# A weight conversion's shift takes its count from a PSUM column

## The chip, the cores and the metric
The kernel runs on one core of a Trainium2 chip. The metric is the device time of one execution in microseconds (us), the median of three runs: 1470.43 (1469.66 to 1470.89).

## The reference
Attention over keys and values that are averaged over 8 positions, then two mixture-like feed-forward blocks without a router. Inputs: q, k, v of 8 x 8 heads x 576 x 64; the weights are 64-bit floats.

```python
k_p = k.reshape(B, H, Sp, 8, D).mean(axis=3)
v_p = v.reshape(B, H, Sp, 8, D).mean(axis=3)
scores = scale * q @ k_p.T ; scores -= max
attn = exp(scores); attn /= sum(attn) + 1e-9
x = attn @ v_p                       # 4608 tokens x 512
h = (x @ w1) * (x @ w2) @ w3         # 1024 wide
x = h @ w_out                        # 512 wide
h = x @ w_in                         # 2048 wide
out = (h / (1 + exp(-1.702 * h))) @ w_out2
```

## The kernel before
Products are made in three passes of a split number (a high and a low half; helpers `split`, lines 103 to 105, and `mm3`, lines 112 to 116). w3 and w_out are multiplied with each other first, so that the first block is (x w1)(x w2) times one matrix.

The weights come as 64-bit floats, read as pairs of 32-bit words, 128 x 512 of them in a tile of 512 KB. `Conv` (line 127) turns them into 32-bit floats: `load` issues the DMA of a tile on SP's queue; `step` (line 155) does one tile: ACT scales the high word (line 166) and the low word (line 168), DVE shifts the high word left by 3 (line 169), POOL adds the two as integers (line 172). Two steps later the tile's `done` runs (a `split`, for w3 behind four turns on TensorE, line 508). There are 72 steps. The first 40 (8 tiles of w_out, 16 of w3, 8 of w1, 8 of w2) write ACT's result into the tile `w` in SBUF (`cv`, four buffers). For the last 32 (w_in and w_out2, from the seventh block on) `self.ps` is set to two PSUM banks, and ACT's result lies there.

The attention runs in groups of two heads, 32 groups. For each: `g0` transposes k and q (lines 255, 256) and sums the keys, `g1` makes the scores (line 277) in two halves, each in a PSUM bank of its own, and subtracts the maximum (lines 282, 284), `g2` is the exponential, `g3` normalizes, `g4` turns the probabilities (for the first four groups on TensorE, lines 351 to 362) and splits them, `g6` makes the outputs (lines 380 to 391). Groups 1 and 3 use the banks acc[2] and acc[3], all others wk[2] and wk[3]: the second half of the scores fills columns 0 to 287 of wk[3], the turning columns 0 to 447, the outputs columns 0 to 287. The row factors of `g3` lie in the last columns of wk[2].

The program order: the loop at line 568 runs step i, then the w3 products of the tile of step i - 3, then from i = 4 on one `tick` of the attention. Counted from 0, with the parts that touch wk[3]: scores of group 0 behind step 5, turning of group 0 behind step 8, scores of group 2 behind step 9, outputs of group 0 behind step 10, turning of group 2 behind step 12, outputs of group 2 behind step 14, scores of group 4 behind step 18. Steps 28 to 39 follow two by two in the loop over f of the first block (line 618), with the scores of groups 5, 6, 7 behind steps 28, 32, 36 and the outputs of groups 4, 5, 6 behind steps 30, 34, 38. Tiles 1, 3, 7, 9 and 12 to 23 are those of w3; from tile 12 on each of them gives 12 products.

Tile order and waits between engines are set by a scheduler that orders each engine's queue by its own forecast, within the dependences that the program order gives. Shifts run on DVE in the order of the steps, so the k-th row of line 169 in time is step k.

Of the kernel before, what the change touches and what calls it, by code (L numbers as in the profile page):

```python
# [9 lines left out]
U32 = mybir.dt.uint32  # L10
I32 = mybir.dt.int32
AF = mybir.ActivationFunctionType
ALU = mybir.AluOpType
# [4 lines left out]
P = 128  # L18
T = 512
# [3 lines left out]
def pooled_attention_moe_moe2(  # L23
# [18 lines left out]
    nc = tc.nc  # L42
# [31 lines left out]
    held = {}  # L74
    acc = [ps_p.tile([P, T], F32, name=f"acc{i}", tag=f"bank{i}") for i in range(4)]
    wk = [ps_p.tile([P, T], F32, name=f"wk{i}", tag=f"bank{i + 4}") for i in range(4)]
    HU = 2 * P
    NP1 = NF2 // 2
    A11, A12, S1, S2, S3, S4, A21, A22 = range(8)
    win_d = [dr_p.tile([P, 8, 2, HU], F32, name=f"wind{f}", tag=f"wind{f}") for f in range(NP1)]  # L80
    wraw_d = [dr_p.tile([P, T], F32, name=f"wrawd{f}", tag=f"wrawd{f}") for f in range(NF2)]
    wu_d = [dr_p.tile([P, NP1, 2, HU], F32, name=f"wud{u}", tag=f"wud{u}") for u in range(8)]
    x2_d = [dr_p.tile([P, KM, T], F32, name=f"x2d{b}", tag=f"x2d{b}") for b in range(NB)]

    def take(shape=(P, 2, T), dtype=F32R):
        pool, i = free.pop(0)
        t = pool.tile(list(shape), dtype, name=f"s{i}", tag=f"s{i}")
        held[id(t)] = (t, pool, i)
        return t
# [5 lines left out]
    def give(*ts):  # L95
        for t in ts:
            if id(t) in held:
                free.append(held.pop(id(t))[1:])
# [28 lines left out]
    class Conv:  # L127
# [27 lines left out]
        def step(self):  # L155

            new = None
            if self.staged:
                t, turn, done = self.staged.pop(0)
                lo_w, hi_w = t[:, :, 0], t[:, :, 1]  # L160
                w = cv_p[0].tile([P, T], F32, name="cv", tag="cv", bufs=4)
                wu = w.bitcast(U32)

                e = self.ps[self.n % len(self.ps)] if self.ps else w
                self.n += 1
                nc.scalar.activation(
                    e, hi_w.bitcast(F32), AF.Prelu, scale=2.0 ** -112, alpha=-2.0 ** 32)
                nc.scalar.activation(lo_w.bitcast(I32), lo_w, AF.Copy, scale=2.0 ** -29)
                nc.vector.tensor_scalar(  # L169
                    out=wu, in0=e.bitcast(U32), scalar1=3, scalar2=None,  # L170
                    op0=ALU.logical_shift_left)
                nc.gpsimd.tensor_tensor(  # L172
                    out=w.bitcast(I32), in0=w.bitcast(I32), in1=lo_w.bitcast(I32), op=ALU.add)
                give(t)
                new = [w, turn, done]
            mid, old = self.line
            if mid and mid[1]:
                mid[0] = mid[1](mid[0])
            key = old[2](old[0]) if old else None
            self.line = [new, mid]  # L180
            self.load()
            return key
# [8 lines left out]
    with pa_ctx:  # L191
# [7 lines left out]
            out=mask[:, 0], in_=mask[:, 0], compare_op=ALU.is_gt, fill=0.0,  # L199
            base=SK, pattern=[[0, D]], channel_multiplier=-1)  # L200
        nc.gpsimd.affine_select(
            out=mask[:, 1], in_=mask[:, 1], compare_op=ALU.is_ge, fill=0.0,
# [8 lines left out]
        for t in s_ts:  # L211
# [6 lines left out]
            out=ident, in_=ident, compare_op=ALU.is_equal, fill=0.0,  # L218
# [244 lines left out]
        def units(f, u0, u1, w, eng):  # L463

            t = take((P, 2, 2, HU))
            v = w.rearrange("p (u m) -> p u m", u=2)
            nc.scalar.copy(t[:, :, 0], v)
            eng.tensor_tensor(out=t[:, :, 1], in0=v, in1=f32(t[:, :, 0]), op=ALU.subtract)
            nc.sync.dma_start(win_d[f][:, u0:u1 + 1], f32(t))
            give(t)  # L470
# [9 lines left out]
        def win_second(f):  # L480
            def done(w):
                h = hold[0]
                a11, a12 = h[:, :HU], h[:, HU:]
                a21, a22 = w[:, :HU], w[:, HU:]
                units(f, A21, A22, w, nc.gpsimd)
# [186 lines left out]
    with tc.tile_pool(name="pb", bufs=1, reuse_waits="tile") as pb, \  # L672
# [16 lines left out]
        def pull():  # L689
            if todo:  # L690
# [3 lines left out]
                if i:  # L694
                    t = pb.tile([P, 2, 2, HU], F32R, name="st", tag=f"st{i}")
                else:
# [219 lines left out]
        for pr in range(1, NPAIR + 1):  # L916
# [122 lines left out]
            for name, u in OUT:  # L1039
# [5 lines left out]
                if pr == NPAIR and name == "M3":  # L1045
# [8 lines left out]
                    for m, t0, n in ((1, 0, T // 2), (0, 0, T), (1, T // 2, T // 2)):  # L1054
                        c = slice(t0, t0 + n)
                        for fp, (g, w) in enumerate(gw):
# [4 lines left out]
                            out=U[m][:, c], in0=bs[m][1][:, c], in1=U[m][:, c], op=ALU.add)  # L1061
                        ts = slice(t0 // 32, (t0 + n) // 32)
                        nc.vector.transpose(
                            out=ot[:, ts, m],
# [74 lines left out]
```

## Time and profile before

| | |
|---|---|
| median of 3 runs | 1470.43 us |
| profiled execution, its own time | 1467.92 us |
| its span | 1466.0 us |
| TensorE (PE) busy | 1433.6 us (98%) |
| VectorE (DVE) busy | 986.1 us (67%) |
| ScalarE (ACT) busy | 694.5 us (47%) |
| GpSimd (POOL) busy | 488.2 us (33%) |
| granted TensorE clock, mean | 0.994 |
| chain that ended last | PE 91%, DVE 4%, POOL 2% |

Busy times are those of one profiled execution. A product's time in a row holds its pipeline, so that TensorE's rows overlap; the sum of an engine's busy time counts each moment once. In a row of the timeline the idle time before an instruction and who ended it stand in brackets.

### The profile page before, as it was taken

To read this page: it belongs to the slowest core of one execution; us is meant where nothing else is said; L and a number is where in the kernel's file an instruction comes from. 1 tells how busy PE (TensorE), PEld (TensorE's weight loads), DVE (VectorE), ACT (ScalarE), POOL (GpSimd) and SP (SyncE) were. 2 spreads that over 40 slices of the span, in tenths; PEclk is the share of its full clock that TensorE was granted. 3 is DMA by queue.
4 is the path that set the end of the run, shared out by engine and by line. 5 is a ranking of instruction groups with operands and counts; after the bars stand their busy time and mean duration, and the time that the engine had idled before them with its cause. 6 is when DMAs were issued, how large, how long until landed. Compare 5 with 4: busy or idle time off the path is not lost.

```text
span 1466.0 us, 19491 instructions
## 1 busy us (share of the span) xinstructions
PE 1433.6 (98%) x6560; PEld 1189.7 (81%) x6560; DVE 986.1 (67%) x1730; ACT 694.5 (47%) x1212; POOL 488.2 (33%) x589
## 2 busy tenths in 40 slices
PE   5979999999999999999999999999999999999998
PEld 4857888888888888888888888888888888888887
DVE  7778998878788887655646336783559354954554
ACT  7875344433333433366635335653455244534442
POOL 8789655554555555347643300000000000000000
PEclk9989999999999999999999999999999999999999
DMA  9992333323222221089869979877677766785665
GB/s 262 245 238 53 60 79 61 80 49 75 52 71 52 71 44 38 27 284 347 324 229 384 349 234 315 305 213 231 201 232 227 230 197 221 242 235 184 199 214 144
DMA packets 294499, 267.64 MB, mean 183 GB/s; under 512 B 201728, under 2 KB 226304, under 8 KB 294400
## 3 DMA queue, kind: packets, MB, share of 16 engines
q1 hardware_dynamic: 291680, 265.09, 60.4%
q10 hardware_dynamic: 2720, 1.31, 0.3%
q8 instruction: 52, 0.85, 0.2%
q14 instruction: 47, 0.39, 0.1%
HBM read 209.72 MB, written 56.62 MB: 182 GB/s over the span
## 4 chain that ended last, share of the span: by engine, by line
PE 91%; DVE 4%; POOL 2%; ACT 1%; DMA 1%; issue 1%; SPq 0%; DVEq 0%; POOLq 0%; ACTq 0%
PE bk L709 45%; PE wk L114 8%; PE wk L115 8%; PE wk L116 8%; PE acc L114 5%; PE acc L115 5%; PE acc L116 5%; PE wk L277 2%; DVE p L314 1%; PE bk L114 1%; PE bk L115 1%; PE bk L116 1%; POOL cv L172 1%; DVE s L105 1%; DVE cv L169 1%
## 5 line engine op out<-in xcount | busy, mean ns | idle before, releaser
L709 PE MATMUL bk<-mv,st 128*128 128x512 f32 (+1 forms) x1164 | 269.8, 385 | 0.0
L709 PE MATMUL bk<-xM,st 128*128 128x512 f32 x1104 | 261.8, 389 | 0.0
L709 PEld LDWEIGHTS bk<-mv,st 128*128 128x128 f32 x1164 | 215.4, 188 | 43.6
L709 PEld LDWEIGHTS bk<-xM,st 128*128 128x128 f32 x1104 | 207.3, 188 | 43.0
L114 PE MATMUL wk<-s,s 128*128 128x512 f32 x576 | 226.9, 396 | 3.4 <-DVE a L641 1.5
L116 PE MATMUL wk<-s,s 128*128 128x512 f32 x576 | 225.1, 392 | 2.1 <-DVE s L105 2.1
L115 PE MATMUL wk<-s,s 128*128 128x512 f32 x576 | 225.0, 391 | 0.0
L314 DVE STREAM_TRANSPOSE p<-s_t 32x160 f32<-32x160 f32 (+1 forms) x560 | 178.5, 319 | 10.3
L114 PE MATMUL acc<-s,s 128*128 128x512 f32 x352 | 134.2, 404 | 8.4 <-DVE s L105 5.4
L115 PE MATMUL acc<-s,s 128*128 128x512 f32 x352 | 140.7, 400 | 1.2 <-POOL s L105 1.1
L116 PE MATMUL acc<-s,s 128*128 128x512 f32 x352 | 140.1, 398 | 0.0
L114 PEld LDWEIGHTS wk<-s,s 128*128 128x128 f32 x576 | 108.4, 188 | 27.1 <-DVE a L641 2.4
L116 PEld LDWEIGHTS wk<-s,s 128*128 128x128 f32 x576 | 108.5, 188 | 24.8 <-DVE s L105 2.3
L115 PEld LDWEIGHTS wk<-s,s 128*128 128x128 f32 x576 | 108.5, 188 | 22.1 <-DVE s L391 0.4
L105 DVE TENSOR_TENSOR mv<-g,mv 128x1024 fp32r<-128x1024 f32 x80 | 97.8, 1222 | 31.0 <-ACT mv L104 29.0
L104 ACT CAST mv<-g 128x1024 fp32r<-128x1024 f32 x80 | 84.2, 1053 | 70.8 <-PE bk L709 70.4
L172 POOL TENSOR_TENSOR cv<-cv,s 128x512 int32<-128x512 int32 x72 | 97.7, 1365 | 28.0 <-DVE cv L169 18.7
L105 POOL TENSOR_TENSOR s<-a,s 128x512 fp32r<-128x512 f32 x56 | 72.3, 1291 | 82.7 <-ACT s L104 62.8
L638 ACT COPY a<-wk 128x512 f32<-128x512 f32 x72 | 42.1, 585 | 110.5 <-PE wk L116 89.9
L369 POOL TENSOR_TENSOR ph<-p,ph 128x576 fp32r<-128x576 f32 x32 | 45.7, 1428 | 128.9 <-ACT ph L368 126.3
L114 PEld LDWEIGHTS acc<-s,s 128*128 128x128 f32 x352 | 67.6, 193 | 23.6 <-ACT s L104 5.1
L115 PEld LDWEIGHTS acc<-s,s 128*128 128x128 f32 x352 | 67.7, 192 | 15.2 <-POOL s L105 2.3
(191 smaller groups left out, 2352.2 us busy)
## 6 DMA issues: line engine op xcount, KB each, us to landing
st<-wud SPq DMA_DIRECT2D x95, 512.0 KB, 4.1
st<-wind SPq DMA_DIRECT2D x70, 512.0 KB, 4.8
st<-wind SPq DMA_DIRECT2D x70, 256.0 KB, 3.9
s<-in_moe_w_dram SPq DMA_DIRECT2D x32, 512.0 KB, 6.4
wind<-s SPq DMA_DIRECT2D x32, 512.0 KB, 5.3
s<-in_moe_w_out_dram SPq DMA_DIRECT2D x24, 512.0 KB, 6.9
kr<-in_k_dram SPq DMA_DIRECT2D x128, 72.0 KB, 2.6
qr<-in_q_dram SPq DMA_DIRECT2D x128, 72.0 KB, 2.6
```

The source lines that it names most:

```text
L104: nc.scalar.copy(dst[:, 0], src)
L105: lo_eng.tensor_tensor(out=dst[:, 1], in0=src, in1=f32(dst[:, 0]), op=ALU.subtract)
L114: nc.tensor.matmul(o, a[:, 0, a_sl], b[:, 0, b_sl], start=first, stop=False)
L115: nc.tensor.matmul(o, a[:, 0, a_sl], b[:, 1, b_sl], start=False, stop=False)
L116: nc.tensor.matmul(o, a[:, 1, a_sl], b[:, 0, b_sl], start=False, stop=last)
L169: nc.vector.tensor_scalar(out=wu, in0=e.bitcast(U32), scalar1=3, scalar2=None, op0=ALU.logical_shift_left)
L172: nc.gpsimd.tensor_tensor(out=w.bitcast(I32), in0=w.bitcast(I32), in1=lo_w.bitcast(I32), op=ALU.add)
L277: nc.tensor.matmul(sc[half][:, i * KW:(i + 1) * KW], qT[:, sl(tt)], mov, start=True, stop=True)
L314: nc.vector.transpose(out=dst[:, :nt, 32 * c:32 * c + 32], in_=s_t[32 * c:32 * c + 32, :nt, 32 * r:32 * r + 32])
L369: nc.gpsimd.tensor_tensor(out=ph[:, 1], in0=s0, in1=f32(ph[:, 0]), op=ALU.subtract)
L638: nc.scalar.copy(a, pa_)
L709: nc.tensor.matmul(o, w[:, x, m], b[:, y], start=first and n == 0, stop=last and n == 2, skip_group_check=True)
```

## The change
Before the first step a column of the PSUM bank wk[3] (column 511) is filled with the integer 3. In the first 40 steps the shift of line 169 becomes an operation of two tensors: the tile in SBUF and this column, read again for all 512 elements. The last 32 steps keep the old form.

```diff
@@ -74,6 +74,8 @@
     held = {}
     acc = [ps_p.tile([P, T], F32, name=f"acc{i}", tag=f"bank{i}") for i in range(4)]
     wk = [ps_p.tile([P, T], F32, name=f"wk{i}", tag=f"bank{i + 4}") for i in range(4)]
+    three = wk[3][:, T - 1:].bitcast(U32)
+    nc.vector.memset(three, 3)
     HU = 2 * P
     NP1 = NF2 // 2
     A11, A12, S1, S2, S3, S4, A21, A22 = range(8)
@@ -166,9 +168,14 @@
                 nc.scalar.activation(
                     e, hi_w.bitcast(F32), AF.Prelu, scale=2.0 ** -112, alpha=-2.0 ** 32)
                 nc.scalar.activation(lo_w.bitcast(I32), lo_w, AF.Copy, scale=2.0 ** -29)
-                nc.vector.tensor_scalar(
-                    out=wu, in0=e.bitcast(U32), scalar1=3, scalar2=None,
-                    op0=ALU.logical_shift_left)
+                if self.ps:
+                    nc.vector.tensor_scalar(
+                        out=wu, in0=e.bitcast(U32), scalar1=3, scalar2=None,
+                        op0=ALU.logical_shift_left)
+                else:
+                    nc.vector.tensor_tensor(
+                        out=wu, in0=e.bitcast(U32), in1=three.to_broadcast([P, T]),
+                        op=ALU.logical_shift_left)
                 nc.gpsimd.tensor_tensor(
                     out=w.bitcast(I32), in0=w.bitcast(I32), in1=lo_w.bitcast(I32), op=ALU.add)
                 give(t)
```

## Rows read from the trace of the kernel before
**Rows 1.** Busy time by stage: stage, its length, busy us by engine, clock, DMA share, GB/s
```profile
0.00:41.86 41.86, 26.32 (x102) 18.21 (x102) 31.49 (x44) 31.60 (x60) 34.66 (x44) 0.92 0.96 267
41.86:102.16 60.30, 53.35 (x271) 43.30 (x272) 45.37 (x79) 50.17 (x107) 46.00 (x53) 0.94 0.99 232
102.16:140.00 37.84, 33.84 (x149) 26.95 (x149) 31.90 (x61) 23.83 (x51) 34.94 (x37) 0.95 0.46 103
140.00:1466.00 1326.00, 1320.12 (x6040) 1101.21 (x6038) 877.37 (x1548) 588.87 (x996) 372.65 (x458) 1.00 0.59 180
```
**Rows 2.** Busy time by stage, the two stretches behind a stop of TensorE
```profile
82.30:87.10 4.80, 4.80 (x12) 3.74 (x13) 4.70 (x10) 4.67 (x11) 4.72 (x5) 0.50 1.31 212
...
108.00:111.50 3.50, 3.50 (x11) 2.82 (x11) 3.50 (x7) 3.50 (x7) 3.13 (x4) 0.55 1.02 241
```
**Rows 3.** Groups of DVE's instructions, 0 to 160 us: busy us, mean ns, idle before
```profile
L169 DVE TENSOR_SCALAR cv<-cv 128x512 uint32<-128x512 uint32 x40 | 34.8, 879 | 9.5 <-ACT cv L166 9.1
...
L641 DVE TENSOR_TENSOR a<-wk,a 128x512 f32<-128x512 f32 x6 | 4.0, 670 | 5.3 <-PE wk L116 5.2
L303 DVE TENSOR_TENSOR s_t<-wk,s_t 128x720 f32<-128x720 f32 x4 | 3.6, 900 | 0.1
```
**Rows 4.** Instructions of line 169, whole span: ns min/median/max, first and last start
```profile
L169 DVE TENSOR_SCALAR cv<-cv x40: 383/716/2794, 5.0 to 137.4; 128x512 uint32<-128x512 uint32 x40
L169 DVE TENSOR_SCALAR cv<-wk x32: 674/682/695, 627.8 to 742.0; 128x512 uint32<-128x512 uint32 x32
```
**Rows 5.** Timeline (start, us, what) around two stops of TensorE
```profile
79.52 1.99 DVE L169 TENSOR_SCALAR cv<-cv 128x512 uint32<-128x512 uint32 x1
79.68 1.27 POOL L172 TENSOR_TENSOR cv<-cv,s 128x512 int32<-128x512 int32 x1
82.27 0.77 PE L114 MATMUL acc<-s,s 128*128 128x512 f32 x1 [3.28 <-DVE s L105]
...
102.35 2.79 DVE L169 TENSOR_SCALAR cv<-cv 128x512 uint32<-128x512 uint32 x1 [0.47 <-ACT cv L166]
107.97 0.80 PE L116 MATMUL wk<-s,s 128*128 128x512 f32 x1 [2.06 <-DVE s L105]
```
**Rows 6.** Timeline: two engines in one PSUM bank, at different columns
```profile
35.44 0.78 PE L356 MATMUL wk<-ident,s_t 128*32 128x128 f32 x3
36.25 0.21 ACT L358 COPY p<-wk 128x64 f32<-128x64 f32 x1 [0.42 <-PE wk L356]
...
111.34 0.35 DVE L391 TENSOR_TENSOR s<-acc,s 128x224 fp32r<-128x224 f32 x1
111.72 0.21 ACT L390 CAST s<-acc 128x64 fp32r<-128x64 f32 x1 [0.18 <-DVE s L391]
```
**Rows 7.** Timeline and chain: shifts 10 to 12, the attention groups, arrivals of q
```profile
28.58 0.95 DVE L169 TENSOR_SCALAR cv<-cv 128x512 uint32<-128x512 uint32 x2
31.41 1.56 DVE L169 TENSOR_SCALAR cv<-cv 128x512 uint32<-128x512 uint32 x1
...
41.86 0.50 PE L114 MATMUL acc<-s,s 128*128 128x512 f32 x1 [0.74 <-DVE s L105]
47.56 0.78 DVE L256 STREAM_TRANSPOSE qT<-qr 128x576 f32<-128x576 f32 x1 [0.18 <-DMA qr<-in_q_dram]
48.85 1.39 PE L277 MATMUL wk<-kbd,qT 128*128 128x144 f32 x10
64.81 0.21 ACT L390 CAST s<-wk 128x64 fp32r<-128x64 f32 x1
74.97 3.73 DMA qr<-in_q_dram
98.79 0.19 ACT L390 CAST s<-wk 128x64 fp32r<-128x64 f32 x1
```
**Rows 8.** Timeline: shift 1 and the first product of its tile
```profile
6.48 0.71 DVE L169 TENSOR_SCALAR cv<-cv 128x512 uint32<-128x512 uint32 x1 [1.04 <-ACT cv L166]
10.68 0.79 PE L114 MATMUL acc<-s,s 128*128 128x512 f32 x1 [0.89 <-ACT s L104]
```

## The prediction
> **What bounds the kernel now.** I read the busy time by stage first [rows 1]. From 140 us to the end TensorE is busy 1320.12 of 1326.00 us: nothing that another engine does there can be worth more than 5.9 us, and the change touches no instruction there (the 32 late conversions keep their old form). So the change is decided in the first 140 us, where TensorE is idle 15.5 us (up to 41.86), 7.0 us (to 102.16) and 4.0 us (to 140), and runs for a while at half clock [rows 1, 2]. In the same stretch the DMA engines are 0.96 and 0.99 busy until 102 us: a weight tile or a q/k block arrives when the queue has got to it, and an engine that gets faster can't pull it forward. DVE and POOL are each busy for over three quarters of it.
>
> Next I looked at the shift itself, line 169. Its 40 early instances (SBUF to SBUF) take 34.8 us of DVE, 879 ns in the mean [rows 3], between 383 and 2794 ns, while the 32 late ones, which read PSUM, lie between 674 and 695 [rows 4]. A form that takes 383 ns when it is alone and up to 2794 at other times is waiting inside its time. The clearest case: a shift begins at 79.52 and ends at 81.51, while POOL's integer add runs from 79.68 to 80.95 [rows 5]. So DVE and POOL stand in each other's way, and that is what the change can remove.
>
> **What it removes and adds, part by part.** (1) *The shift's duration.* The trace has no shift of two tensors. From below it is bounded by the free old form, 0.38 us [rows 4], from above by a product of two tensors with a broadcast PSUM operand and 720 elements, 0.90 us [rows 3]. Nearest is line 641, two tensors of 512 elements with one operand in PSUM and one in SBUF: 0.67 us in the mean; the late shift from PSUM has the same 0.68 [rows 3, 4]. I take 0.68: 40 x (0.88 - 0.68) = 8 us less of DVE.
>
> (2) *What of that lies on the path.* DVE is not the bound, so the 8 us count only where TensorE waits. Two of its idle spells end with a line-105 subtraction that stood behind a long shift [rows 5]: at 82.27 (3.28 us idle; the shift was 1.99 long, 1.3 over 0.68) and at 107.97 (2.06 us idle; the shift was 2.79 long, 2.1 over). Together 3.4 us. Behind the 107.97 stop TensorE ran 3.5 us at a granted clock of 0.55, that is mostly at the lower of its two levels, 1.2 of 2.4 GHz (it had idled just before); without the stop that gives back 3.5 x 0.45 = 1.6 us [rows 2]. Sum of the gain if nothing is added: 5.0 us. From below it is zero, if the new shift waits for POOL as well.
>
> (3) *The memset* of one column stands at the head of the kernel, where DVE has nothing to do until the first weight tile has landed: nothing. Without that cover it would be one instruction, below the 0.38 us of the shortest shift [rows 4]. No instruction of the stage writes column 511 of wk[3] (score products fill 288 columns, turned probabilities 448, attention outputs 288).
>
> (4) *The new operand's bank.* This is the part that costs. The count lies in wk[3], the bank into which the attention groups 0, 2, 4, 5, 6, 7 write half of their scores and outputs. The rows say that this kernel orders accesses of two engines by bank and not by column. ACT's copy of columns 0 to 63 of wk[3] (line 358) began only behind line 356's products into columns 64 to 447 [rows 6]; and ACT's copy of the last 64 columns (line 390) waited at 111.72 for DVE's read of the 224 columns before them, though the two share no byte [rows 6]. So every early shift will wait for whatever TensorE and ACT were given to do in wk[3] earlier in program order. On DVE it stands at the head of a queue in which everything behind it waits as well: line 105's halves, the maxima of the scores, the transposes; behind those wait TensorE's products.
>
> Program order says which shift stands behind what: shift 6 behind the scores of group 0, shift 9 behind its turning, shift 10 behind the scores of group 2, shift 11 behind the outputs of group 0, shift 13 behind the turning of group 2, shift 15 behind its outputs, shift 19 behind the scores of group 4, shift 29 behind those of group 5. Now the conversions run far ahead of the attention: shifts 10 and 11 are at 28.58, shift 12 at 31.41, but the scores of group 2 at 48.85, because their q landed only at 47.5 [rows 7]. That arrival is DMA, so it stays. Shift 10 thus moves from 28.6 to about 50.3 (48.85 plus 1.4 of products).
>
> What waits: shift 12 feeds the first of the twelve w3 tiles that give 12 products each, and from there TensorE is dense (41.86 on [rows 7]). Shift 12 now stands behind the outputs of group 0, which stand behind shift 10. From below: three shifts in a row, 50.3 + 2 x 0.68 = 51.7. From above: the last copy of group 0's outputs is where it was, 64.81 [rows 7], plus 0.2 and one shift: 65.7. Group 0 was held up by conversions on the same queues, so I take 56.2. From the start of a shift to the first product of its tile a free pipeline took 4.2 us (6.48 to 10.68 [rows 8]). So the dense stage starts at 60.4 instead of 41.86 (ends: 55.9, 69.9).
>
> The stage from 41.86 to 102.16 holds 53.35 us of TensorE [rows 1]. Less 4.8 x 0.5 = 2.4 for its stretch at half clock [rows 2] and about 4 for attention work of groups 0 to 2 that now fits before it: 47. New waits inside it: shifts 13, 15 and 19 open only one after the other; the q of group 4 lands at 78.7 [rows 7], so shift 19 at some 82, when tiles 15 to 18 still keep TensorE busy. I put 3 us for the hand-overs. 60.4 + 47 + 3 = 110.4, where it was 102.16: 8.2 us later.
>
> Against it: from 102.16 to 140 TensorE lost 4.0 us idle and 1.6 at low clock [rows 1, 2]; as w1 and w2 are in SBUF by then, part of this 5.6 comes back. I take half, 2.8. **Sum: 8.2 - 2.8 = 5.4, or 5 us slower.** The profiled execution took 1467.92 us (span 1466.0 plus 1.9 around it), 2.5 under the median of 1470.43; I add to the median: 1475.5. The ends of the cost: with 55.9 as start, no hand-overs and all 5.6 given back, 55.9 + 47 - 102.2 - 5.6 = -5; with 69.9, 6 of hand-overs and nothing given back, 69.9 + 53 - 102.2 = +21.
>
> *The skill on the same point.* The Trainium skill's page "PSUM — Partial Sum Buffer", section "PSUM bank collisions raise a hardware error", says that two engines must not be in one bank and one group of 32 partitions at once, whatever the columns, and that software has to keep them apart by bank. By that rule the sum is the one above; if columns were enough, part (4) fell away and part (2) alone, 5.0 us of gain, would be left. The trace agrees with the page: line 390's wait of 0.18 us at 111.72. The page "SBUF — State Buffer", section "Who interferes with whom", says that a DVE operation in a two-port mode and any GpSimd operation lock each other out for a whole instruction, and that an operation with one SBUF input outside those modes doesn't; the 1.99 us shift agrees, and part (2) is the gain by it.
>
> **The rivals.** *Lock gone, coupling hidden (faster).* The attention fills the DVE, ACT and POOL time that the held conversions leave, its groups keep step with the shifts, and the w3 stage ends where it did because it waited for accumulators and arrivals anyway (7.0 us idle in it). For it: TensorE had 22 us of idle time before 102. Against: shift 10 moves by over 20 us and the DMA order doesn't. Time: 1470.4 - 5.0 = 1465.4. The point from which this decides: dense stage starting before 56.
>
> *Even.* The dense stage starts 18.5 later, but the hand-overs cost nothing and all 5.6 of the later loss come back: 8.2 - 3 - 5.6 = -0.4, 1470.
>
> *Attention as late as now (much slower).* The outputs of group 2 stay where they are, with their last copy at 98.79 [rows 7]; shift 15 then opens at 99, and nine tiles (15 to 23) follow, each of 12 products and 4 turns at 53.35/271 us [rows 1], 3.15 us: 99 + 4 + 28 = 131 instead of 102, less 5.6: +23, 1494. Against: what delayed them were the conversions in the same queues.
>
> *It doesn't do what it says.* The new form still waits for POOL: line 641 speaks against it, with 0.67 us in the mean where POOL is as busy [rows 3]. Then part (4) has no gain beside it: also slower, 1478.
>
> **How the numbers follow.** 0.2% of 1470 is 2.9 us, about what a measurement of this kernel can tell from no change. Slower by the coupling (forecast, own range 1473.4 to 1483; the shift that still waits for POOL is counted here): 0.42; much slower: 0.11; even: 0.21; faster: 0.26. The range reaches from the gain of part (2) to near the upper end of part (4): 1464.5 to 1489.
>
> **What would show it.** Line 169 with two tensors at 0.66 to 0.70 us, without a tail, and 27 us in all: part (1). Shift 10 behind the line-277 products of group 2, near 50 us, and DVE or POOL waits put down to PE or ACT on wk: part (4). First w3 tile's products near 60. TensorE idle time up to 102 near 30 us where it was 22.5. Wrong, if shifts still run 20 us ahead of the attention (no ordering by bank), or if the q of group 2 lands much before 47 (the DMA order moved).

## The result, and the profile after

The changed kernel takes 1489.41 us (median of 4 runs, 1485.92 to 1491.66) where the kernel before takes 1470.05 beside it (1469.07 to 1470.89): 19.4 us slower, a ratio of 1.0130 (95% interval 1.0109 to 1.0151). The forecast was 1475.5, with a range up to 1489.0: slower was right, the size was not, and the time lies 0.4 us above the range. The rival that came nearest was "attention as late as now", 1494, to which I had given 11 in 100. Lines below are those of the changed kernel (the shift is line 176 there, the low-word scaling 170, the load of a weight tile 153, the products of split numbers 116 to 118, the scores 284, the outputs 387 to 398); the profiled execution took 1491.66 us.

The page's head and the busy time by stage, in the stages of [rows 1]; then the stages that fit the new course (length, busy us by engine with counts, clock, DMA share, GB/s):

```profile
span 1489.9 us, 19484 instructions
PE 1442.1 (97%) x6560; PEld 1195.3 (80%) x6560; DVE 973.9 (65%) x1731; ACT 698.2 (47%) x1212; POOL 481.7 (32%) x589
...
0.00:41.86 41.86, 22.91 (x82) 15.90 (x82) 23.66 (x41) 31.66 (x59) 25.98 (x38) 0.88 0.98 268
41.86:102.16 60.30, 38.92 (x162) 29.07 (x162) 34.34 (x65) 34.85 (x82) 35.56 (x51) 0.71 0.82 193
102.16:140.00 37.84, 36.60 (x177) 30.58 (x177) 27.33 (x57) 25.90 (x48) 28.39 (x35) 0.97 0.50 141
140.00:1489.90 1349.90, 1343.68 (x6141) 1119.74 (x6139) 888.59 (x1571) 605.78 (x1026) 391.76 (x466) 1.00 0.58 177
...
0.00:60.00 60.00, 30.10 (x113) 21.48 (x114) 32.15 (x56) 40.32 (x79) 34.05 (x50) 0.80 0.97 267
60.00:82.00 22.00, 18.55 (x89) 14.02 (x87) 14.43 (x24) 14.61 (x34) 11.29 (x16) 0.93 0.83 166
82.00:102.50 20.50, 13.23 (x46) 9.49 (x46) 11.75 (x26) 11.92 (x30) 16.53 (x24) 0.54 0.72 157
```

From 41.86 to 102.16 TensorE is busy 38.92 us where it was 53.35, at a mean clock of 0.71 instead of 0.94. The time went into two stops: before 60 us, where it idles 29.9 us (15.5 in the kernel before), and from 82 to 102.5, where it idles 7.3 us (1.6) and works at 0.54, mostly at 1.2 GHz. From 140 us on nothing is lost. In the whole span TensorE idles 47.8 us instead of 32.4, and its busy time is 1442.1 instead of 1433.6 us, which fits the products that ran at the lower clock behind each stop: 15.4 + 8.5 = 23.9 us, the difference of the two spans. (The median differs by 19.4; the profiled run was the longest of the four.)

The shifts, first the 40 early ones of the whole span (ns min/median/max), then where they stand (start, us; x4 is four shifts merged):

```profile
L176 DVE TENSOR_TENSOR cv<-cv,wk x40: 648/680/690, 5.5 to 195.5; 128x512 uint32<-128x512 uint32 x40
```
```profile
23.97 1.88 DVE L176 TENSOR_TENSOR cv<-cv,wk 128x512 uint32<-128x512 uint32 x3
33.42 0.68 DVE L176 TENSOR_TENSOR cv<-cv,wk 128x512 uint32<-128x512 uint32 x1
46.64 2.61 PE L284 MATMUL wk<-kbd,qT 128*128 128x144 f32 x10
50.54 0.68 DVE L176 TENSOR_TENSOR cv<-cv,wk 128x512 uint32<-128x512 uint32 x1
61.06 1.27 DVE L176 TENSOR_TENSOR cv<-cv,wk 128x512 uint32<-128x512 uint32 x2
64.67 1.28 DVE L176 TENSOR_TENSOR cv<-cv,wk 128x512 uint32<-128x512 uint32 x2 [0.23 <-ACT p L366]
94.63 0.21 ACT L397 CAST s<-wk 128x64 fp32r<-128x64 f32 x1
95.60 2.47 DVE L176 TENSOR_TENSOR cv<-cv,wk 128x512 uint32<-128x512 uint32 x4
98.12 1.33 PE L284 MATMUL wk<-kbd,qT 128*128 128x144 f32 x4 [1.11 <-DVE cv L176]
```

The form does what it says: 0.65 to 0.69 us and no tail, where the old one went from 0.38 to 2.79 [rows 4]. But shift 10, at 28.6 before [rows 7], is at 50.54, behind the scores of group 2; shifts 11 and 12 follow the outputs of group 0 at 61.06, shift 13 the turning of group 2 at 64.67, with 14 behind it, and 15 to 18 open together at 95.60, behind the last copy of the outputs of group 2 (94.63). The tie works the other way too: at 98.12 the scores into columns 0 to 287 of wk[3] wait 1.11 us for shifts that read its column 511. The last of the 40 is at 195.5 instead of 137.4 [rows 4].

The waits before the copies of group 0's outputs (55.83 to 60.70) and of group 2's (until 94.63), by the timeline; then what held the loads of weight tiles on SP's queue up to 140 us (total, times, longest), three rows of the changed kernel and the two longest of the kernel before:

```profile
52.41 0.65 ACT L170 ACTIVATE s<-s 128x512 int32<-128x512 uint32 x1 [2.58 <-DMA s<-in_moe_w_dram]
54.58 0.65 ACT L170 ACTIVATE s<-s 128x512 int32<-128x512 uint32 x1 [1.32 <-DMA s<-in_moe_w_dram]
55.83 0.38 ACT L397 CAST s<-wk 128x288 fp32r<-128x288 f32 x1
...
76.92 0.66 ACT L170 ACTIVATE s<-s 128x512 int32<-128x512 uint32 x1 [5.18 <-DMA s<-in_moe_w_dram]
80.92 0.73 POOL L331 TENSOR_TENSOR va<-vr 128x256 f32<-128x256 f32 x1 [7.72 <-DMA vr<-in_v_dram]
81.75 0.54 PE L387 MATMUL wk<-ph,vm 128*128 128x288 f32 x2 [2.34 <-ACT ph L375]
85.54 0.61 PE L388 MATMUL wk<-ph,vm 128*128 128x288 f32 x1 [3.25 <-POOL ph L376]
92.40 0.76 DVE L398 TENSOR_TENSOR s<-wk,s 128x288 fp32r<-128x288 f32 x2 [5.35 <-ACT s L397]
```
```profile
SPq L153 <- PE acc L118: 8.4, 4, 3.0
SPq L153 <- ACT cv L168: 5.4, 1, 5.4
SPq L153 <- POOL cv L179: 4.6, 3, 2.4
```
```profile
SPq L151 <- ACT s L104: 1.4, 1, 1.4
SPq L151 <- POOL s L105: 0.4, 1, 0.4
```

Twice ACT waits at the head of its queue for the low word of a weight tile that has not landed, with the attention's copies and splits queued behind it: 2.58 and 1.32 us ahead of group 0's outputs, 5.18 us ahead of group 2's; POOL waits 7.72 us for the next group's v with `ph` of group 2 behind it. And the loads of weight tiles now wait for slots that held tiles and unfinished products don't give back (18.4 us in these three rows; 1.8 in the two of the kernel before), with the loads of q, k and v behind them in SP's queue. The first of tile 12's products, the last product of the w3 stage (the 192nd on acc), and TensorE between the two; then the last product of that stage in the kernel before:

```profile
69.89 0.49 PE L116 MATMUL acc<-s,s 128*128 128x512 f32 x1
...
135.64 0.39 PE L118 MATMUL acc<-s,s 128*128 128x512 f32 x1
...
69.89:136.03 66.14, 55.58 (x250) 44.81 (x249) 42.62 (x87) 39.62 (x82) 48.37 (x67) 0.85 0.64 156
```
```profile
101.76 0.40 PE L116 MATMUL acc<-s,s 128*128 128x512 f32 x1
```

So the w3 stage ends at 136.0 us instead of 102.16. That is 33.9 us later, with 28 more matmuls of other work done by then (401 against 373 in all).

### The profile page after: what moved, and what is told of

The parts are those of the page before. It is cut to its first block, busy times and chain, and to the rows that moved or that the text cites. A ratio compares the mean times of both kernels' runs of the same rounds, so it can differ in the third digit from the quotient of the medians.

```text
span 1489.9 us, 19484 instructions
## 1 busy us (share of the span) xinstructions
PE 1442.1 (97%) x6560; PEld 1195.3 (80%) x6560; DVE 973.9 (65%) x1731; ACT 698.2 (47%) x1212; POOL 481.7 (32%) x589
## 4 chain that ended last, share of the span: by engine, by line
PE 88%; DMA 4%; SPq 3%; DVE 2%; ACT 1%; issue 1%; POOL 0%; ACTq 0%; DVEq 0%; POOLq 0%
PE bk L716 41%; PE wk L118 9%; PE wk L117 9%; PE wk L116 9%; PE acc L118 5%; PE acc L116 5%; PE acc L117 5%; PE wk L284 2%; SPq L236 2%; DMA s<-in_moe_w_dram 2%; DMA wud<-wt 1%; PE bk L116 1%; PE bk L117 1%; PE bk L118 1%; PE wk L390 1%
## 5 line engine op out<-in xcount | busy, mean ns | idle before, releaser
L179 POOL TENSOR_TENSOR cv<-cv,s 128x512 int32<-128x512 int32 x72 | 95.6, 1343 | 30.2 <-DVE cv L172 16.8
```

Source lines behind the costliest of these rows:

```text
L179: nc.gpsimd.tensor_tensor(out=w.bitcast(I32), in0=w.bitcast(I32), in1=lo_w.bitcast(I32), op=ALU.add)
```

## The experiments

**The theory:** the tie of the shift to the attention's bank holds the shifts back and makes the loss; the form itself gains a little. **Rivals:** the two-tensor form makes the loss (its duration, its waits on the chip); or any edit makes it, because the scheduler then plans all queues anew. In some runs every queue is held to the order of another kernel, so that only the instructions differ; these are called "held to an order". All times are medians of 4 runs unless said, with the ratio to runs of the kernel before on the same chip (1469.7 to 1470.4).

**1. A read of the bank beside the old shift** (the edits here and below are shortened; this one is shown against the changed kernel).

```diff
-        tensor_tensor(out=wu, in0=e, in1=three.to_broadcast([P, T]), op=logical_shift_left)
+        if not self.ps: nc.vector.tensor_copy(peek[0], three)
+        tensor_scalar(out=wu, in0=e, scalar1=3, op0=logical_shift_left)
```

> The old shift by a constant, and ahead of each early one a DVE copy of the one column of wk[3] to SBUF: the tie to wk[3] without the two-tensor form. If the tie to the attention's bank makes the loss: 1483 to 1494, with shift 10 near 50 and shift 15 near 95 us. If the two-tensor form or its duration makes it: 1468 to 1474 (40 short copies of some 0.06 us on DVE, which is not the bound).

1480.63 us, 1.0067 (1.005 to 1.0084), outside what either theory said. This was no test of the tied shift: the copy and the shift don't depend on each other, so the shifts ran ahead as before (shift 10 at 28.8 us), and the copies, 5.8 us of DVE in all, came late. The 10 us that it lost stand in a new order of the queues, with its stops at 100 to 140 us (15.4 us idle there; the kernel before idled 4.0 from 102.16 on). It speaks for the last rival, an edit that holds no shift back costs 10 us too, but not cleanly: the copies themselves are tied to the bank (copy 10 is at 56.2 us).

**2. The count in SBUF**, the two-tensor form with no tie; and the old shift held to that run's order.

```diff
-    three = wk[3][:, T - 1:].bitcast(U32)
+        three[0] = pa.tile([P, 1], U32, name="three")
```

> The two-tensor shift with its count in an SBUF column: the form without the tie to wk[3]; both operands now lie in SBUF. If the tie makes the loss: 1465 to 1474 and shift 10 back near 28 us. If the form makes it: 1483 or more. The shift's duration: 0.68 us if the form alone sets it, about 0.9 in the mean with a tail up to 2 us if two SBUF operands bring POOL's interference back.

> The kernel before, with every engine's queue held to the order of the run that had the count in SBUF (there 1483.7 us, no tie, shifts of 1.35 us in the mean). If those 13 us came from the long shifts: 1468 to 1474. If planning the order anew costs that much by itself: 1478 to 1484.

1483.74 us, 1.0090 (1.0075 to 1.0105), and with the old shift in the same order 1478.72, 1.0053 (1.0038 to 1.0068). The shift by an SBUF column, ns min/median/max, and a pair of them beside POOL's work:

```profile
L174 DVE TENSOR_TENSOR cv<-cv,three x40: 664/1093/4049, 5.4 to 158.9; 128x512 uint32<-128x512 uint32 x40
```
```profile
92.06 6.07 DVE L174 TENSOR_TENSOR cv<-cv,three 128x512 uint32<-128x512 uint32 x2
92.49 1.28 POOL L177 TENSOR_TENSOR cv<-cv,s 128x512 int32<-128x512 int32 x1
```

So with both operands in SBUF the form is slower than the old one (1353 ns in the mean against 1121 in the same order), and that costs 1483.7 - 1478.7 = 5 us. The other 8.4 us are neither tie nor form: a new order of the queues alone cost them, as the last rival has it, with no shift tied.

**3. The old shift in the changed kernel's order, and the tie without the form.** The second keeps the old shift for 511 columns and shifts only the last one by the count in wk[3]:

```diff
+    nc.vector.tensor_scalar(out=wu[:, :T - 1], in0=e[:, :T - 1], scalar1=3, ...)
+    nc.vector.tensor_tensor(out=wu[:, T - 1:], in0=e[:, T - 1:], in1=three, ...)
```

> The kernel before, each instruction as it was (shift by a constant, SBUF to SBUF, no count in PSUM), but every engine's queue is held to the order that the changed kernel has. Theory: the tie does its harm through the order, since a shift that stands in DVE's queue behind the scores' maxima can't run ahead, tied or not; then 1486 to 1493. Rival: the loss comes from waits of the new instruction on the chip (its operand in PSUM, its semaphores) that the order alone doesn't bring; then 1468 to 1478.

> The old shift for 511 of the 512 columns and the two-tensor form with the count in wk[3] for the last column alone: the tie without the form for the bulk; the order is planned anew. If the tie makes the loss: 1484 to 1496, with the one-column shift of tile 10 near 50 us and of tile 15 near 95. If the form's duration makes it: 1468 to 1474 (40 operations of one column, some 0.1 us each).

1494.24 us, 1.0159 (1.0143 to 1.0176), and 1493.70, 1.0153 (1.0138 to 1.0168). Shifts 10, 11 and 12, and 15 to 18, of the first; then the one-column shifts 10, 11 and 12, and 15 to 18, of the second:

```profile
51.04 0.42 DVE L169 TENSOR_SCALAR cv<-cv 128x512 uint32<-128x512 uint32 x1
59.52 0.75 DVE L169 TENSOR_SCALAR cv<-cv 128x512 uint32<-128x512 uint32 x2
...
93.43 5.41 DVE L169 TENSOR_SCALAR cv<-cv 128x512 uint32<-128x512 uint32 x4
```
```profile
50.91 0.15 DVE L179 TENSOR_TENSOR cv<-cv,wk 128x1 uint32<-128x1 uint32 x1
59.88 0.21 DVE L179 TENSOR_TENSOR cv<-cv,wk 128x1 uint32<-128x1 uint32 x2
...
95.13 0.34 DVE L179 TENSOR_TENSOR cv<-cv,wk 128x1 uint32<-128x1 uint32 x4
```

These two settle the question of the form. The untied old shift, made to stand where the changed kernel puts it, loses 24 us; and 40 tied shifts of a single column, 4.8 us of DVE in all, bring the whole loss. The form is not the cause: it makes the same order faster by 4.8 us (1494.2 to 1489.4; the runs don't overlap). One place to see it: shifts 15 to 18 take 5.41 us in the old form and 2.47 in the new one.

**4. A bank free of the attention up to shift 32**: groups 0, 2, 4 and 5 use wk[2] for both halves; with the new shift, with the old shift planned anew, and with the old shift held to the order of the first.

```diff
-            return acc[2:] if n < NPE and n % 2 else wk[2:]
+            return acc[2:] if n < NPE and n % 2 else ([wk[2], wk[2]] if n < 6 else wk[2:])
```

> The changed kernel, but the attention groups 0, 2, 4 and 5 use wk[2] for both their halves, one after the other, so that nothing but the count lies in wk[3] while the early shifts run. If the tie makes the loss: 1464 to 1472, shift 10 back near 28 us; what stays is the gain of the shorter shift less what the serial halves cost (some 1 to 2 us per group). If the form makes it: 1483 or more.

> The kernel before with the same two halves in wk[2], as the control of the run with the free bank: 1470 to 1473 (groups 0, 2, 4 and 5 lose 1 to 2 us each, partly hidden). Its difference to the run with the new shift and the free bank is the gain of the shorter shift; from the stalls behind long shifts I expect 2 to 5 us, from a shift that hinders nothing on the path 0.

> The run with the free bank and the new shift (1498.0 us) with the old shift in its place and the same order in every queue: nothing differs but the shift's form, and there is no tie in either. The gain of the shorter shift by itself: if my step (2) holds, 2 to 5 us, so 1500 to 1503 here; if the longer shift hinders nothing, 1498.

1497.99 us, 1.0188 (1.0173 to 1.0204); 1501.24, 1.0204 (1.0189 to 1.0219); 1498.34, 1.0194 (1.0179 to 1.0209). My expectation for the control was wrong by 30 us: with halves one after the other in a bank, or with the new order that this brings, the kernel is far dearer than by 1 to 2 us a group, so this layout says nothing on the tie. Nor is it free of it: groups 6 and 7 still use wk[3], shift 33 comes at 166.5 us behind group 6 (112.1 in the control), and the scores of group 7 wait for the shifts:

```profile
166.53 2.47 DVE L176 TENSOR_TENSOR cv<-cv,wk 128x512 uint32<-128x512 uint32 x4
169.15 1.30 PE L284 MATMUL wk<-kbd,qT 128*128 128x144 f32 x4 [10.54 <-DVE cv L176]
```

Only the first and the third can be compared, and there the shorter shift gained 0.4 us, which is nothing. That TensorE does not wait for a long shift in this order is my reading of it.

**5. ACT's queue.** The changed kernel held to its own order, but for the 30 of 40 low-word scalings that stood ahead of their own tile's line 168: they stand right behind it.

> The changed kernel with every queue held to its own order, but for ACT's: the 30 low-word scalings that stood there ahead of their own tile's line-168 step stand right behind it. If the hold of ACT's queue by scalings that wait for a weight tile's DMA (22.2 us of waits up to 170 us) delays the attention and with it shift 15: outputs of group 2 some 10 us earlier (shift 15 near 85 instead of 95.6) and 1476 to 1484. If those waits lie beside the others: 1487 to 1491.

1486.90 us, 1.0121 (1.0104 to 1.0138). Shifts 15 to 18:

```profile
91.42 2.47 DVE L176 TENSOR_TENSOR cv<-cv,wk 128x512 uint32<-128x512 uint32 x4
```

They open 4.2 us earlier and not 10, shifts 11 and 12 open 4.8 us earlier (56.2 and 56.8), and the time falls by 2.5 us, inside the intervals. So ACT's hold was one of several; most of group 2's delay is elsewhere (POOL still waits 6.73 us for v there, and the outputs of group 1 still stand behind a run of w3 products on TensorE).

**6. Half of the shifts each.** Two-tensor form up to shift 14 only, or from 15 on only.

```diff
-                if self.ps:
+                if self.ps or self.n > 15:     # the other run: self.n <= 15
```

> The two-tensor form for shifts 0 to 14 alone, the old form from shift 15 on. If the tie makes the loss gate by gate: the idle stretch at 40 to 60 us stays and the one at 82 to 102 goes, 1476 to 1484. If the form makes it: in proportion, 15 of 40, 1477. If planning anew is all: anywhere from 1470 to 1490, without the idle stretch at 40 to 60.

> The old form for shifts 0 to 14, the two-tensor form from shift 15 on. If the tie makes the loss gate by gate: the stretch up to 60 us is that of the kernel before, shift 15 waits for the outputs of group 2 and an idle stretch of 10 to 20 us stands before 100 us, 1480 to 1490. If only the early gates count: 1466 to 1473.

1486.97 us, 1.0116 (1.0101 to 1.0131), and 1482.62, 1.0088 (1.0073 to 1.0103). TensorE's stages, first those of the run up to 14, then of the run from 15 on:

```profile
40.00:60.00 20.00, 11.10 (x41) 8.43 (x41) 11.61 (x22) 11.87 (x27) 8.75 (x14) 0.59 0.94 257
...
80.00:100.00 20.00, 18.33 (x89) 14.05 (x87) 11.03 (x20) 13.30 (x34) 17.34 (x23) 0.91 0.98 220
...
120.00:140.00 20.00, 14.60 (x59) 11.39 (x58) 19.05 (x28) 13.92 (x29) 17.97 (x18) 0.91 0.41 78
```
```profile
60.00:80.00 20.00, 9.90 (x37) 6.56 (x35) 9.58 (x18) 11.62 (x28) 7.82 (x12) 0.50 0.97 218
80.00:100.00 20.00, 14.93 (x59) 11.98 (x59) 15.47 (x29) 10.48 (x25) 16.29 (x21) 0.62 0.78 140
100.00:120.00 20.00, 20.00 (x105) 16.98 (x104) 17.43 (x41) 14.33 (x29) 18.87 (x27) 1.00 0.54 171
```

Each gate makes its own stop: the early ones that before 60 us, shift 15 (here at 86.7 us) that before 100. But the parts don't add up, 17.0 + 12.7 against 19.4: the first run has a new stop at 120 to 160 us (9.0 us idle), where no shift is tied. A later start is in part given back, and each plan has stops of its own.

**7. The distance in program order.** The attention's steps start at step 12 or 20 of the first loop, instead of 4, so that a shift stands behind accesses that are older by 8 or 16 steps; each with the new shift and with the old one, and the old one held to the order of the first.

```diff
-            if i >= 4 and tick_n[0] < 20:
+            if i >= 12 and tick_n[0] < 20:
```

> The changed kernel with the attention's steps placed 8 conversion steps later in program order (the first loop starts them at its step 12 instead of 4): the count stays in wk[3], but shift k now stands behind accesses that lay 8 steps earlier, shift 18 behind the scores of group 2, shift 23 behind its outputs. If the tie to earlier accesses makes the loss: shifts 6 to 14 free, and 1464 to 1478. If the form or any new planning makes it: 1483 or more.

> The kernel before with the attention's steps 8 conversion steps later in program order, old shift, no tie; planned anew. The control of the run with the count in wk[3] and the same place of the steps (1482.6 us). If the tie still costs there: 1470 to 1476, so that 7 to 12 us are the tie's. If that loss is the later place of the attention or the new plan: 1480 to 1486.

> The old shift held to the order of that run (1482.6 us) in every queue: the form alone, for the third time after 4.8 us in the changed kernel's order and 0.4 us in the order with the free bank. If the shorter shift pays where TensorE waits for DVE: 1484 to 1488. If it pays nothing: 1482.6.

> The changed kernel with the attention's steps started at step 20 of the first loop instead of 4: only shift 22 and those behind it stand behind any access of the attention to wk[3]. If the distance in program order decides: no shift up to 21 is held; with the control of the old shift at the same place the difference is below 5 us, or a gain of up to 5 (the shorter shift). If the form or new planning makes the loss: some 15 us over that control.

> The control of the run before it: the kernel before with the attention's steps started at step 20, old shift, no tie. The attention comes later than in the kernel before: 1470 to 1490; what counts is the difference to the run with the two-tensor shift.

| attention starts at step | new shift | old shift, own plan | old shift, the new one's order |
|---|---|---|---|
| 4 | 1489.41 | 1470.05 | 1494.24 |
| 12 | 1482.63 (1.0091; 1.0074 to 1.0109) | 1487.00 (1.0110; 1.009 to 1.0129) | 1486.68 (1.0121; 1.0105 to 1.0137) |
| 20 | 1483.80 (1.0094; 1.0079 to 1.0109) | 1487.40 (1.0120; 1.0105 to 1.0135) | |

With every queue planned anew the new shift loses 19 us to the old one where the attention stands close ahead of it, and is 4 us better where it stands 8 or 16 steps further off. At step 12 the order of the tied kernel is as good as the untied one's (1486.7 and 1487.0 with the old shift): there the tie costs nothing, and the 4 us are the form's. Shift 10 is at 26.0 us there and shift 12 at 30.0, as free as before (28.6 and 31.4 [rows 7]). But the later shifts are held there too. Shift 23, tied to the outputs of group 2, in the run with the new shift, then in its control:

```profile
104.23 1.87 DVE L176 TENSOR_TENSOR cv<-cv,wk 128x512 uint32<-128x512 uint32 x3
```
```profile
65.29 0.41 DVE L169 TENSOR_SCALAR cv<-cv 128x512 uint32<-128x512 uint32 x1
```

It stands 39 us later, and the w3 stage ends at 114.3 instead of 91.6, yet up to 102.5 us TensorE idles 25.3 us against 22.1 (in the changed kernel 40.6, in the kernel before 22.5). So a held shift is not a loss in itself; it is one where TensorE stops for it. What fills TensorE's time there no run took apart. The intervals of a pair overlap by a little, so the 4 us are good to some 2; that they have one sign in three pairs is what I rest on. Neither place beats the kernel before: with the attention later the old shift, too, loses 17 us.

**8. The part that needs no new order.** The new form for the first 8 shifts, the count in acc[3], held to the order of the kernel before.

```diff
-    three = wk[3][:, T - 1:].bitcast(U32)
+    three = acc[3][:, T - 1:].bitcast(U32)
-                if self.ps:
+                if self.ps or not (self.n <= 8):
```

> The kernel before in its own order, with the two-tensor shift for the first 8 tiles alone and the count in column 511 of acc[3], which no attention step touches ahead of them in program order: the part of the change that needs no new order. If the shorter shift pays early: those 8 shifts take 5.4 us instead of the 9.5 they took (two of 0.92 each in a pair of 1.84, and 0.43 to 1.53), the first products come earlier by up to 2 us and 1468 to 1469.5. If TensorE waits there for weight tiles and not for DVE: 1470, no change.

1471.03 us (12 runs), 1.0013 (1.0005 to 1.0022). The eight shifts take 5.4 us, as expected, and gain nothing. TensorE's longest waits up to 30 us are for POOL's adds (total, times, longest), here and then in the kernel before:

```profile
PE wk L515 <- POOL cv L179: 10.1, 2, 8.7
```
```profile
PE wk L508 <- POOL cv L172: 10.1, 2, 8.7
```

They are as long as before. So no version faster than both was found.

## Why the prediction was right or wrong

**Step (1), the duration: right.** 0.68 us forecast, 0.68 measured, 26.2 us in all (forecast 27).

**Step (2), 5.0 us gained if nothing is added: near in size, in other orders.** 4.8, 4.1 and 0.4 us at equal order, 4.4 and 3.6 in the pairs planned anew, each good to some 2. The two stops in the kernel before that it was worked out from were not tried by a run, so it is not shown that the gain falls just where TensorE stands behind a long shift; the order where it was nothing fits that.

**Step (3), the memset: right.** One instruction of 0.06 us at 0.9 us.

**Step (4), the tie: right in kind, wrong in size.** Shift 10 was forecast at 50.3 and came at 50.54. The step that failed is the sum behind it: start of the dense stage, its work, its hand-overs, and what comes back later.

| term | forecast | measured |
|---|---|---|
| shift 12 (bounds 51.7 to 65.7) | 56.2 | 61.7 |
| from there to the first product of its tile | 4.2 | 8.2 |
| the w3 stage from there, 47 of work and 3 of hand-overs | 50 | 66.1 |
| its end, against 102.16 | 110.4, 8.2 late | 136.0, 33.9 late |
| given back by the end of the span | 2.8 | 10.0 |
| sum | 5.4 | 23.9 (the median: 19.4) |

The **start** was 9.5 us late. For the outputs of group 0 I took a value in the middle of its bounds, with the reason that the conversions no longer stood in their way. They did: low-word scalings that waited for their tiles stood ahead of the copies on ACT, and with them moved (run 5) shift 12 came at 56.8. The other 4.0 us stand on TensorE: the tile's four turns were done by 65.4, but the turns of two more tiles and the scores of group 3 came ahead of its first product, at 69.89.

The **hand-overs** are the worse term, over by 16.1 us together with the work. TensorE is idle 10.6 of the 66.1 us where I had put 3. Of the 55.6 us in which it is busy some 7 are the price of the lower clock (an estimate: 13.2 us at 0.54 from 82 to 102.5, 32.6 at 0.97 behind it), which leaves 48.5, near the 47. I let shift 19 open at some 82 us; shift 15 opened at 95.6 and shift 19 at 103.0. The rival "attention as late as now" was nearer there (99, and 131 for the end of the stage), and my reason against it was wrong: a held shift does not clear the queues for the attention. It fills the four `cv` buffers, so the next tiles keep their slots, so SP's loads wait, and q, k and v behind them. The DMA share from 41.86 to 102.16 fell from 0.99 [rows 1] to 0.82, while I had taken the arrivals as fixed. (This chain is read off the trace's waits; no run tried its links. Run 5 tried ACT's hold, which is another.)

What is **given back** was too low by 7.2 us, in part because the 28 matmuls that stand before the stage's end already need not be done behind it. The prediction's own upper end of the cost, +21, would have held the 19.4; that is luck, as two terms lay far above their upper ends (10.6 us of idle time against 6, and a clock price that was not in the sum) and one far below (10 us given back against none).

**What I had left out: the plan.** I kept every other instruction in its place. The scheduler orders all queues anew, and the new order is where the loss sits: with it the untied old shift is as slow (run 3). Part of that order is forced, a tied shift can't stand ahead of what it must follow; part is a plan made for a forecast that the chip doesn't keep, such as the 30 low words ahead of their tiles, worth 2.5 us at most, which is inside the noise. A plan with no tie at all cost 8.4 us (run 2), and later places of the attention cost 17 with none (run 7). So of the 24 us some 8 or more may be the plan rather than the tie; how much is not settled. Shown is that the loss sits in the order and not in the form (run 3), that a tie of one column without the form brings the same held shifts and the same loss (run 3), and that each half of the tied shifts makes a stop of its own (run 6). That the tie is the whole cause is not shown: with the attention further off the same form, still holding shifts, lost nothing to its control, and no run has the PSUM form without its tie while the attention stands where it stood.

**The bank, and POOL.** By the Trainium skill's page "PSUM — Partial Sum Buffer" (section "PSUM bank collisions raise a hardware error") the columns don't matter and the bank does; the 1.11 us at 98.12 and shift 10's 22 us agree with it. By the Trainium skill's page "SBUF — State Buffer" (section "Who interferes with whom") an operation of DVE with two SBUF inputs contends with a GpSimd instruction that reads SBUF; run 2 agrees, with 1353 ns in the mean where the PSUM column gave 679.

## What to carry to other kernels

An operand parked in an idle corner of a PSUM bank is not free: whoever reads it is ordered behind everything that the program gave to the bank before, so ask first how far ahead of that work the reader runs now, and what TensorE has to do while the reader is held (run 7: the same tie at no cost). In a kernel whose queues are planned, cost the new order and not the moved instruction alone: hold the old instructions to the new order and run that, and the form and the order come apart in one experiment. A term whose only support is that "the queue will be free then" belongs at its upper bound, and a stop of TensorE is priced with the slow products behind it.

## What was not expected of the hardware and the plan

A two-tensor shift of 128 x 512 took 0.65 to 0.69 us with its second operand a PSUM column, and 0.66 to 4.05 us with it in SBUF beside POOL's work: where the one column lies decides. And the kernel's time is sensitive to its order: of the 14 orders of the queues that ran here, that of the kernel before is the fastest, and the others lie 8 to 31 us above it with the old shift or the new one. (Some of these programs also differ in bank layout or in the place of the attention; the 8.4 us of run 2 are the order alone.)
